# One of two attention output tiles goes to the shared PSUM banks, and four operand tiles of the channel mixing become float32 tiles

## The chip, the cores and the metric

The kernel runs on one core of one Trainium2 chip. The metric is the device time of one execution in microseconds. Before the change the median of three runs is 569.63 us (568.62 to 572.48).

## The reference

Two steps follow each other. The first is an attention without softmax in which weights decay with distance; `lam` is one decay factor per head. The second mixes over the positions ("token mixing") and then over the features ("channel mixing").

```python
# q, k, v: (4 batches, 8 heads, 768 positions, 64), block of 64 positions
for b in range(nb):
    intra = einsum('bhic,bhjc->bhij', qb, kb) * Dmask      # lam ** (i - j) below the diagonal
    intra = einsum('bhij,bhjd->bhid', intra, vb)
    inter = einsum('bhic,bhcd->bhid', qb * lam_pow, kv_state)
    out[:, :, sl] = intra + inter
    kv_state = lam_block * kv_state + einsum('bhsd,bhse->bhde', kb * rev_pow, vb)

x  = out as (4, 768, 512)
h  = maximum(x.transpose(0, 2, 1) @ w_tok1, 0) @ w_tok2    # 768 -> 256 -> 768
u  = x + h.transpose(0, 2, 1)
h2 = maximum(u @ w_ch1, 0) @ w_ch2                         # 512 -> 1536 -> 512
return u + h2
```

All is float32. Where the kernel multiplies float32 matrices on TensorE in the faster fp32r type, it splits each operand into a high and a low part and adds three products.

## The kernel before

**Order.** There is one program, and each engine works through its own list of instructions in the order in which the Python code writes them. An instruction that must wait stops all that stand behind it on its engine. Tiles that bear the same tag in a pool share a fixed number of buffers in turn: a new tile takes the buffer that was taken longest ago, and its first write waits until the last reader of that buffer's previous tile is done. Nothing else sets the order.

**Attention (the loop at L618 to L700).** A pair is one batch and two heads; there are 16 pairs, and iteration `i` of the loop runs from -2 to 15. A sequence of 768 positions is six chunks of 128, and most tiles hold three chunks, so that each step comes as halves `g` = 0 and 1. On TensorE (PE) the iteration has, in this order:

- the scores of pair i+1 (`sc`, L287);
- the outputs of pair i, first half (`xT`, L314 for the weights times v, L324 for the part from the running state), which ScalarE (ACT) copies to `uT` at L331;
- the products k·v of pair i+1 (`kv`, L254), from which VectorE (DVE) makes the running states at L262 in one scan (`sv`);
- the outputs of pair i, second half (`xT` again);
- the transposes of k of pair i+2 in two tiles (`kt`, L211), copied by ACT at L216, and for the first pairs those of q (`qt`, L228, copied by ACT at L229); later pairs' q is transposed by DVE at L221;
- groups of the token mixing that are ready (`ph` L446, `pu` L467), and between them the outputs of pair i transposed back (`xp`, L346) and split by ACT (`xhi`, L354) and DVE (`xlo`, L355).

Between these the queue `waiting` puts steps that read weights in and split them; one such chain runs ACT L377, L378, DVE L379, L380, L383, ACT L390 for a piece.

**PSUM banks.** `bank` (L105) gives a tile with one of three tags: `sc` has four buffers, `xT` one, `sh` three. `kv`, `kt`, `qt`, `xp`, `ph` and `pu` take `sh` in turn; both halves of the outputs take the only `xT`.

**Channel mixing (L1256 to L1399).** It runs over n = 0 to 17 (three rounds of six), with seven products each (`product`, L783, into PSUM banks `a`, `b`, `d`; at L797 TensorE writes them). After a product comes its `drain` (L820): ACT and DVE take the bank, add, apply the maximum, and make pairs of operand tiles, a high and a low part (`hi_of` on ACT, at L812; `low_of` on DVE, at L808; `low_sum` on GpSimd (POOL), at L818). The second weight matrix is applied by `mm2` (L998) in the first round, and by `half` (L1037, products `gb` and `gc` at L1052) in the other two. POOL also splits second weights (`c2hx`, `c2lx`, at L1127) and operands (`o3l` to `o7l`, at L583, shared with DVE).

Two queues hand out tiles there, first in, first out: `tiles` holds operand tiles (fp32r), which `hi_of` takes in pairs and `half` gives back; `temps` holds float32 tiles for sums on the way (`snap`, `e` of L837, `temp`), which are given back by `give`. Which tile of a queue an instruction uses depends on how many are in it. All tiles stand in SBUF.

Of the kernel before, what the change touches and what calls it, by code (L numbers as in the profile page):

```python
# [9 lines left out]
F32 = mybir.dt.float32  # L10
F32R = mybir.dt.float32r
# [14 lines left out]
def kernel(  # L26
# [28 lines left out]
    P = 128  # L55
# [6 lines left out]
    CB = 512  # L62
# [8 lines left out]
    def later(n, at_end=False):  # L71
        left = 0 if at_end and len(waiting) < 8 else 1 + (n > 2)
        n += len(waiting) > 7
        for _ in range(min(n, len(waiting))):
            left -= waiting[0] in acts
            if left < 0 and n < 99:
                break
            waiting.popleft()()
# [26 lines left out]
    def bank(tag, nm, n):  # L105
        return ps.tile([P, n], F32, tag=tag, bufs={"sc": 4, "xT": 1, "sh": 3}[tag], name=nm)
# [199 lines left out]
    def outputs(i, g):  # L306
        b, p = pairs[i]
        st = stb[i % 2]
        xT = bank("xT", f"xT{i}{g}", 3 * P)
        for cg in range(3):  # L310
            c = 3 * g + cg
            cs = slice(cg * P, (cg + 1) * P)
            for h in range(2):
                nc.tensor.matmul(  # L314
                    out=xT[h * D : (h + 1) * D, cs],
                    lhsT=vns[i][:, h, c, :],
                    rhs=weights_of[i, g, h][:, cg, :],
                    start=(cg == 0),
                    stop=False,
                )  # L320
            if c == 0:
                continue
            for h in range(2):
                nc.tensor.matmul(  # L324
                    out=xT[h * D : (h + 1) * D, cs],
                    lhsT=st[:, c - 1, h, :],
                    rhs=qss[i][:, c - 1, :],
                    start=False,
                    stop=(cg == 2),
                )  # L330
        nc.scalar.copy(out=uT[b][:, p, 3 * g * P : (3 * g + 3) * P], in_=xT)  # L331
# [286 lines left out]
    for i in range(-2, NI):  # L618
# [8 lines left out]
        if i >= 0:  # L627
            outputs(i, 0)
# [3 lines left out]
        if i >= 0:  # L632
            outputs(i, 1)
        if i + 2 < NI:
            turn_q(i + 2)
        if i in loads:
            x = loads.index(i)
# [43 lines left out]
        if i in turns:  # L681
            x = turns.index(i)
# [84 lines left out]
    def flush():  # L767
        for f in todo.popleft() if todo else []:
            f()
# [13 lines left out]
    def product(n, s):  # L783

        r, g = divmod(n, NG)
        o = PROD[s]
        ch, cl = c1s[n]
        oh, ol = ops[r, o]
        c = c_of.setdefault(n, {})
        into = {1: "b", 2: "a", 6: "b", 7: "d", 5: "b", 3: "b", 4: "d"}[o]  # L790
        if into not in c:
            c[into] = bank("sc", f"{into}{n}", CB)
        first = o in (1, 2, 7)
        i = 0
        for ct in range(2):
            for w, x in ((ch, oh), (cl, oh), (ch, ol)):
                nc.tensor.matmul(  # L797
                    out=c[into], lhsT=w[:, WI[o], ct], rhs=x[:, ct], start=(first and i == 0), stop=(i == 5),
                    skip_group_check=True,
                )  # L800
                i += 1

    tiles, temps, ring, G = deque(), deque(), deque(), {}
# [178 lines left out]
    def mm2(n, x, t):  # L982

        r, g = divmod(n, NG)
        if n < NG:
            c2h, c2l = c2s[n]
            cs = slice(t * P, (t + 1) * P)
            po = bank("sh", f"po{n}{x}{t}", CB)
        else:
            w2 = W[n, t // 2]  # L990
            c2h, c2l = w2[:, 0], w2[:, 1]
            cs = slice(t % 2 * P, (t % 2 + 1) * P)
            po = list(G.values())[(4 * x + t) % 4]
        i = 0
        for jj in range(JG):
            hh, hl = hs[n, jj, x]
            for w, h in ((c2h, hh), (c2l, hh), (c2h, hl)):
                nc.tensor.matmul(out=po, lhsT=w[:, jj, cs], rhs=h, start=(i == 0), stop=(i == 3 * JG - 1), skip_group_check=n >= NG)  # L998
                i += 1
            if t == 3 and n >= NG:  # L1000
                tiles.extend((hh, hl))
        if n >= NG and x == 0 and t % 2 == 1:
            spent(n, t // 2)
        return lambda: gather(n, x, t, po)
# [197 lines left out]
    def later2(n):  # L1202
        for _ in range(min(n, len(fuse))):
            if fuse[0]() is False:
                break
            fuse.popleft()
# [16 lines left out]
    def convert(g, i):  # L1223
        at = dict(name=f"wa{g}{i}")
        if len(pieces) % 3 == 0:
            a = wp.tile([P, 4 * FG], U32, tag="wa", bufs=1, **at)
        else:
            a = fp.tile([P, 4 * FG], F32, tag="fa", bufs=2, **at).bitcast(U32)
        fresh[g, i] = a.bitcast(F32)
        t = wp.tile([P, 4 * FG], U32, tag="t", bufs=1, name=f"t{g}{i}")  # L1230
        waiting.extend(convert_piece(fresh[g, i, 0], a, signs, t))
        waiting.append(lambda: converted.add((g, i)))
# [9 lines left out]
    def next_piece():  # L1242
        if pieces:
            raw_of(*pieces[0])
# [11 lines left out]
    for n in range(NQD):  # L1256
        r, g = divmod(n, NG)
        for s in range(7):
# [22 lines left out]
            if n == 0:  # L1281
# [12 lines left out]
                if s == 0:  # L1294
                    p2.close()
                    hp = ctx.enter_context(tc.tile_pool(name="hp", bufs=3, reuse_waits="tile"))
# [12 lines left out]
            if n < NG:  # L1309
                for q_ in range(s, s + 1 if s < 6 else 8):  # L1310
                    if q_ == s:
                        product(n, s)
                        flush()
                        later(1)
                        later2(2)
                        if sums:
                            sums.popleft()()
                        drain(n, s)
                    add = mm2(n - 1, 1 - q_ // 4, q_ % 4)
                    flush()  # L1320
                    later(1)
                    later2(2)
                    add()
                    if n < NG and pieces:
                        if tick in turn_at:
                            convert(*pieces.popleft())
                        if tick - 2 in turn_at:
                            next_piece()
                        tick += 1
            else:  # L1330
                if n == NG and s == 0:
                    tasks.extend(lambda q_=q_: mm2(NG - 1, 1 - q_ // 4, q_ % 4) for q_ in range(8))
                if n == NG and s == 1:
                    for i in range(4):
                        x = tp.tile([P, 2, CB], F32R, tag="tt", bufs=4, name=f"tt{i}")
                        tiles.extend((x[:, 0], x[:, 1]))
                if n == NG + 1 and s == 1:
                    for i in range(3):
                        for t in ("hh0", "hl0", "hh1", "hl1"):
                            tiles.append(hp.tile([P, CB], F32R, tag=t, name=f"{t}x{i}"))  # L1340
                    for t in ("c2h", "c2l"):
                        x = w2b.tile([P, JG, DM], F32R, tag=t, name=f"{t}x")
                        ring.append(x.rearrange("p a (j e) -> p a j e", j=JG))
                    pump()
                    for t in range(2):
                        G["b", t] = bank("sh", f"gb{t}", CB)
                    G["c", 0] = bank("sh", "gc0", CB)
                    G["c", 1] = bank("xT", "gc1", CB)
                if n % 2 and n < NQD - 2 and s == 2:
                    tasks.extend(lambda o=o, i=i, d=n // 2: half(d, o, i) for o in ORDER for i in range(2))  # L1350
                if n == NQD - 1 and s == 0:
                    tasks.extend(lambda q_=q_: mm2(NQD - 2, 1 - q_ // 4, q_ % 4) for q_ in range(8))
                if r == 1 and n % 2 == 0 and s == (0 if n == NG else 3):
                    take_raw(n // 2)
                    fuse.extend(sums_of_weights(n // 2))
                product(n, s)
                flush()
                if sums:
                    sums.popleft()()
                drain(n, s)  # L1360
                later2(1)
                k = (1, 1, 2, 1, 2, 1, 2)[s] if n == NQD - 1 else 1
                for _ in range(k):
                    add = tasks.popleft()() if tasks else lambda: None
                    flush()
                    later2(1)
                    add()
                    if todo_out:
                        todo_out.popleft()()
# [4 lines left out]
        if n == NG - 1:  # L1374
# [8 lines left out]
            for t in ("c2h", "c2l"):  # L1383
                x = wa.tile([P, JG, DM], F32R, tag=t, name=f"{t}x")
# [42 lines left out]
```

## Time and profile before

| what | value |
|---|---|
| median of the runs | 569.63 us (568.62 to 572.48) |
| the profiled execution, its own time | 567.56 us |
| its span in the trace | 565.8 us, so 1.76 us lie around it |
| PE busy in the span | 541.0 us (96%) |
| DVE, POOL, ACT busy | 387.8, 285.4, 247.3 us |
| mean granted TensorE clock | 0.995 of full speed |

The times of the trace count from the start of the span. A row of the timeline gives the start, the busy time, the engine, the line, the operation, the tile written and the tiles read, the shape, how many instructions it groups, and in brackets how long the engine stood idle before and what ended that. In a table of windows the columns are the window, then per engine the busy time with the number of instructions in brackets (PE, its weight loads, DVE, ACT, POOL), the granted clock, the DMA share and GB/s. Weight loads run beside matmuls, so that PE busy and PE weight loads overlap.

### The profile page before, as it was taken

Reading aid. Unit: us, or ns where it says so; the run is one execution under the profiler, and the core shown is the slowest. Engines: PE = TensorE matmul, PEld = TensorE weight load, DVE = VectorE, ACT = ScalarE, POOL = GpSimd, SP = SyncE. Lnnn points to the kernel's source line nnn. Section 1 sums busy time; section 2 is a strip of 40 time slices with the busy share of each in tenths; the row PEclk is TensorE's granted clock in tenths of the full one; section 3 lists DMA queues with packets and bytes.
Section 4 is the critical chain, followed back from the end, with each engine's and each line's share of the span. In section 5 each row is a group of like instructions: output and inputs, shape, how many; then the busy total and the mean of one; then the engine's idle time right before and its main releaser. Section 6 shows DMA issues by size and latency. Waiting matters only on the chain.

```text
span 565.8 us, 9630 instructions
## 1 busy us (share of the span) xinstructions
PE 541.0 (96%) x3686; PEld 459.9 (81%) x3686; DVE 387.8 (69%) x590; ACT 247.3 (44%) x449; POOL 285.4 (50%) x240
## 2 busy tenths in 40 slices
PE   5987989999999999999999999999998999999996
PEld 4877879988998988888888878888876888888884
DVE  4747776676684787888896667389479765575463
ACT  3456543453524546456445344343465334332111
POOL 6746548345324287667639753385788223131000
PEclk9989999999999999999999999999999999999999
DMA  9999887199630158687587999868536797653007
GB/s 183 248 228 209 189 192 170 30 228 216 133 71 2 74 205 311 221 286 279 189 294 238 259 213 252 308 218 311 181 104 223 156 234 280 240 182 137 0 3 146
DMA packets 163726, 108.12 MB, mean 191 GB/s; under 512 B 136800, under 2 KB 147552, under 8 KB 163680
## 3 DMA queue, kind: packets, MB, share of 16 engines
q1 hardware_dynamic: 153648, 87.31, 58.6%
q10 hardware_dynamic: 10032, 20.19, 9.7%
q8 instruction: 29, 0.48, 0.3%
q14 instruction: 17, 0.14, 0.1%
HBM read 75.50 MB, written 31.98 MB: 190 GB/s over the span
## 4 chain that ended last, share of the span: by engine, by line
PE 81%; DVE 6%; ACT 4%; issue 2%; DMA 2%; SPq 1%; POOL 1%; ACTq 1%; DVEq 0%; POOLq 0%
PE b L797 16%; PE po L998 11%; PE gb L1052 9%; PE d L797 8%; PE gc L1052 6%; PE ph L446 6%; PE pu L467 5%; PE a L797 4%; PE xT L314 4%; PE sc L287 3%; PE xT L324 2%; PE gb L998 2%; PE gc L998 2%; DMA qn<-in_q_dram 1%; PE xp L346 1%
## 5 line engine op out<-in xcount | busy, mean ns | idle before, releaser
L275 POOL COPY stb<-sv 64x320 f32<-64x320 f32 x32 | 25.4, 793 | 50.7 <-DVE sv L262 49.7
L314 PE MATMUL xT<-a,vn 128*64 128x128 f32 x384 | 37.1, 285 | 5.2 <-ACT uT L331 5.2
L331 ACT COPY uT<-xT 128x384 f32<-128x384 f32 x32 | 15.4, 480 | 55.5 <-PE xT L324 55.5
L1011 DVE TENSOR_TENSOR uT<-po,uT 128x512 f32<-128x512 f32 x48 | 32.6, 683 | 10.2 <-PE po L998 10.0
L998 PE MATMUL po<-hh,c2l 128*128 128x512 f32 x96 | 37.7, 393 | 0.0
L998 PE MATMUL po<-hl,c2h 128*128 128x512 f32 x96 | 37.6, 392 | 0.0
L998 PE MATMUL po<-hh,c2h 128*128 128x512 f32 x96 | 37.6, 391 | 0.0
L300 DVE TENSOR_TENSOR a<-sc,mask 128x384 f32<-128x384 f32 x64 | 32.1, 543 | 4.9 <-PE sc L287 4.9
L324 PE MATMUL xT<-qs,stb 128*64 128x128 f32 x320 | 32.0, 278 | 0.0
L818 POOL TENSOR_TENSOR tt<-t,tt 128x512 fp32r<-128x512 f32 x13 | 16.8, 1296 | 29.1 <-ACT tt L812 27.2
L314 PEld LDWEIGHTS xT<-a,vn 128*64 128x64 f32 x384 | 22.7, 139 | 9.3 <-ACT uT L331 6.0
L1067 DVE TENSOR_TENSOR uT<-gb,uT 128x512 f32<-128x512 f32 x40 | 26.1, 683 | 3.8 <-PE gb L1052 3.8
L446 PE MATMUL ph<-xhi,w1h 128*128 128x256 f32 x96 | 28.2, 294 | 0.3 <-DVE hl L451 0.3
L355 DVE TENSOR_TENSOR xlo<-xp,xhi 128x384 fp32r<-128x384 f32 x32 | 17.7, 554 | 14.7 <-ACT xhi L354 14.6
L287 PE MATMUL sc<-qT,kT 64*128 64x128 f32 x384 | 26.5, 286 | 0.8 <-DVE qT L221 0.5
L446 PE MATMUL ph<-xlo,w1h 128*128 128x256 f32 x96 | 27.1, 283 | 0.0
L446 PE MATMUL ph<-xhi,w1l 128*128 128x256 f32 x96 | 27.1, 283 | 0.0
L287 PEld LDWEIGHTS sc<-qT,kT 64*128 64x128 f32 x384 | 23.4, 193 | 3.9 <-issue 1.7
L525 POOL TENSOR_TENSOR c1l<-wa,c1h 128x512 fp32r<-128x512 f32 (+1 forms) x12 | 18.7, 1569 | 15.6 <-ACT c1h L522 15.6
L818 POOL TENSOR_TENSOR hl1x<-t,hh1x 128x512 fp32r<-128x512 f32 x12 | 16.8, 1404 | 18.9 <-ACT hh1x L812 18.3
L241 POOL TENSOR_TENSOR qs<-qT,lamp 128x640 f32<-128x640 f32 x16 | 25.4, 1589 | 0.0
L797 PE MATMUL b<-o,c1h 128*128 128x512 f32 x72 | 25.2, 391 | 0.0
(359 smaller groups left out, 1724.8 us busy)
## 6 DMA issues: line engine op xcount, KB each, us to landing
c1h<-k SPq DMA_DIRECT2D x12, 896.0 KB, 5.6
c1l<-k SPq DMA_DIRECT2D x12, 896.0 KB, 8.1
raw<-in_moe_w_ch_dram SPq DMA_DIRECT2D x7, 1024.0 KB, 6.0
kn<-in_k_dram SPq DMA_DIRECT2D x32, 192.0 KB, 4.5
vn<-in_v_dram SPq DMA_DIRECT2D x16, 384.0 KB, 5.8
k<-c1h ACTq DMA_DIRECT2D x6, 896.0 KB, 3.6
k<-c1l ACTq DMA_DIRECT2D x6, 896.0 KB, 4.2
out_dram<-y SPq DMA_DIRECT2D x80, 64.0 KB, 2.4
```

The source lines that it names most:

```text
L287: nc.tensor.matmul(out=sc[h][:, c * P : (c + 1) * P], lhsT=kTs[i][r, cs], rhs=qTs[i][r, cs], start=True, stop=True,)
L300: nc.vector.tensor_mul(out=a, in0=scored[i, g][h].rearrange("p (c i) -> p c i", i=P), in1=mask[:, 2 * p + h, None, :].broadcast_to([P, 3, P]),
L314: nc.tensor.matmul(out=xT[h * D : (h + 1) * D, cs], lhsT=vns[i][:, h, c, :], rhs=weights_of[i, g, h][:, cg, :], start=(cg == 0), stop=False,)
L324: nc.tensor.matmul(out=xT[h * D : (h + 1) * D, cs], lhsT=st[:, c - 1, h, :], rhs=qss[i][:, c - 1, :], start=False, stop=(cg == 2),)
L446: nc.tensor.matmul(out=ph, lhsT=w[:, c, fs], rhs=x[:, c], start=(i == 0), stop=(i == 3 * NC - 1))
L467: nc.tensor.matmul(out=pu, lhsT=h[:, kk, cs], rhs=w[:, kk, ss], start=(i == 0), stop=(i == 3 * NK - 1))
L797: nc.tensor.matmul(out=c[into], lhsT=w[:, WI[o], ct], rhs=x[:, ct], start=(first and i == 0), stop=(i == 5), skip_group_check=True,)
L818: nc.gpsimd.tensor_sub(out=B_[key][1], in0=src, in1=B_[key][0].bitcast(F32))
L998: nc.tensor.matmul(out=po, lhsT=w[:, jj, cs], rhs=h, start=(i == 0), stop=(i == 3 * JG - 1), skip_group_check=n >= NG)
L1011: nc.vector.tensor_add(out=ub, in0=two(po), in1=ub)
L1052: nc.tensor.matmul(out=G[into, t], lhsT=w2[:, v, j, t * P : (t + 1) * P], rhs=x, start=(o in (5, 1, 2) and not second and i == 0), stop=(i ...
L1067: nc.vector.tensor_add(out=ub, in0=two(G[into, t]), in1=ub)
```

## The change

Two places change. The second half of a pair's outputs takes a buffer of `sh` in place of the `xT` buffer. And of the twelve tiles with tags `hh0`, `hl0`, `hh1`, `hl1` that are added in the channel mixing at n = 7, the last four go as float32 tiles to `temps` in place of fp32r tiles to `tiles`. `tiles` then hands out 16 operand tiles in place of 20 from there on, `temps` 13 in place of 9.

```diff
     def outputs(i, g):
         b, p = pairs[i]
         st = stb[i % 2]
-        xT = bank("xT", f"xT{i}{g}", 3 * P)
+        xT = bank("sh" if g else "xT", f"xT{i}{g}", 3 * P)
...
                 if n == NG + 1 and s == 1:
                     for i in range(3):
                         for t in ("hh0", "hl0", "hh1", "hl1"):
-                            tiles.append(hp.tile([P, CB], F32R, tag=t, name=f"{t}x{i}"))
+                            at = dict(tag=t, name=f"{t}x{i}")
+                            if i < 2:
+                                tiles.append(hp.tile([P, CB], F32R, **at))
+                            else:
+                                temps.append(hp.tile([P, CB], F32, **at))
```

Every engine has the same instructions in the same order as before; what changes is the buffers they use and with that what they wait for. The first place is TensorE in iteration 2, from the end of `kv3` on: `xT21` is the second half of pair 2's outputs, `kt40` and `kt41` the transposes of k of pair 4, `qt40` the first of q. In brackets stand the semaphores that a first instruction waits for. Before:

```order
L254 MATMUL kv3_517<-vn3_351,kd3_459 64x64 x8
L314 MATMUL xT21_534<-a210_406,vn2_233 64x128 [waits Activation_49]
...
L324 MATMUL xT21_534<-qs2_375,stb0_111 64x128 x2
L211 MATMUL kt40_550<-ident_61,kn4_353 128x128 [waits DMAHW7_49,DMAHW6_49,DVE_49]
L211 MATMUL kt40_550<-ident_61,kn4_353 128x128 x2
L211 MATMUL kt41_555<-ident_61,kn4_353 128x128 [waits DVE_49]
L211 MATMUL kt41_555<-ident_61,kn4_353 128x128 x2
L228 MATMUL qt40_560<-ident_61,qn4_354 128x128 [waits DMAHW1_49,DMAHW0_49,DVE_49]
```

And now:

```order
L254 MATMUL kv3_517<-vn3_351,kd3_459 64x64 x8
L314 MATMUL xT21_534<-a210_406,vn2_233 64x128 [waits DVE_49]
...
L324 MATMUL xT21_534<-qs2_375,stb0_111 64x128 x2
L211 MATMUL kt40_550<-ident_61,kn4_353 128x128 [waits DMAHW7_49,DMAHW6_49,DVE_49]
L211 MATMUL kt40_550<-ident_61,kn4_353 128x128 x2
L211 MATMUL kt41_555<-ident_61,kn4_353 128x128 [waits DVE_49]
L211 MATMUL kt41_555<-ident_61,kn4_353 128x128 x2
L228 MATMUL qt40_560<-ident_61,qn4_354 128x128 [waits DMAHW1_49,DMAHW0_49,Activation_49]
```

`xT21` no longer waits for ACT, which copies the first half out of the `xT` bank. With one more tile in the turn of `sh`, each tile behind it takes another buffer: of the three buffers in use before `kv3`, `xT21` takes the one that stood first in line for `kt40`, `kt40` the one that stood next, `kt41` that of `kv3` itself (whose reader is the scan `sv3` on DVE), and `qt40` that of `xT21` (whose reader is ACT's copy).

The second place is DVE in iteration n = 11 of the channel mixing, at its sum `e` (L837), with `d11` the bank of a product. Before:

```order
L1069 TENSOR_TENSOR uT_60<-uT_60,gc1_3912 128x512 [waits DVE_49,PE_49]
L583 TENSOR_TENSOR o7l2_4527<-uT_60,o7h2_4526 128x512 [waits Activation_49]
L837 TENSOR_TENSOR snap1_3667<-d11_4498,t1_3661 128x512 [waits DMAHW0_49,DMAHW6_49,Activation_49,Pool_49]
L808 SCALAR_TENSOR_TENSOR t0_3660<-snap1_3667,t0_3660 128x512 [waits DVE_49]
L583 TENSOR_TENSOR o5l2_4552<-uT_60,o5h2_4551 128x512 [waits PE_49,Activation_49]
L808 SCALAR_TENSOR_TENSOR hl0x2_3904<-snap1_3667,hh0x2_3903 128x512
```

And now:

```order
L1069 TENSOR_TENSOR uT_60<-uT_60,gc1_3912 128x512 [waits DVE_49,PE_49]
L583 TENSOR_TENSOR o7l2_4527<-uT_60,o7h2_4526 128x512 [waits Activation_49]
L837 TENSOR_TENSOR t0_3660<-d11_4498,snap0_3666 128x512 [waits DVE_49,Activation_49]
L808 SCALAR_TENSOR_TENSOR hl0x2_3904<-t0_3660,hl0x2_3904 128x512 [waits DVE_49,Pool_49]
L583 TENSOR_TENSOR o5l2_4552<-uT_60,o5h2_4551 128x512 [waits PE_49,Activation_49]
L808 SCALAR_TENSOR_TENSOR tt2_3707<-t0_3660,tt2_3707 128x512
```

The sum `e` writes another tile, `t0` in place of `snap1`, and no longer waits for POOL or for DMA queues; the rows around it stand in the same order.

## The prediction

> **What bounds the kernel now.** I read the page's busy shares and chain first, then a table of windows to see where TensorE stands idle, then the list of TensorE's waits, then the timeline at each.
>
> ```profile
> PE 541.0 (96%) x3686; PEld 459.9 (81%) x3686; DVE 387.8 (69%) x590; ACT 247.3 (44%) x449; POOL 285.4 (50%) x240
> ...
> PE 81%; DVE 6%; ACT 4%; issue 2%; DMA 2%; SPq 1%; POOL 1%; ACTq 1%; DVEq 0%; POOLq 0%
> ```
>
> ```profile
> 31.60:130.00 98.40, 88.58 (x1081) 81.08 (x1078) 69.19 (x117) 50.02 (x101) 54.70 (x52) 0.98 0.84 175
> ...
> 184.00:413.00 229.00, 228.75 (x1030) 189.34 (x1030) 172.27 (x238) 109.29 (x185) 144.74 (x109) 1.00 0.73 239
> 413.00:440.00 27.00, 24.82 (x106) 19.23 (x105) 22.48 (x30) 16.23 (x31) 22.49 (x15) 1.00 0.48 161
> ```
>
> TensorE is busy for 541.0 of 565.8 us, so all idle time together is 24.8 us, the most that taking waits away can give. Of that 98.40 - 88.58 = 9.8 lies in the attention and 27.00 - 24.82 = 2.2 where the change of the queues acts. From 184 to 413 it is idle for 0.25 of 229: what TensorE gains before, it keeps there.
>
> ```profile
> PE xT L314 <- ACT uT L331: 5.2, 4, 2.1
> ...
> PE gc L1052 <- DVE hl0x L808: 1.0, 1, 1.0
> PE gb L1052 <- DVE uT L1067: 0.6, 1, 0.6
> PE gc L1052 <- DVE tt L808: 0.5, 1, 0.5
> ```
>
> The first edit aims at 5.2 us in four stalls; the second touches the stretch of the other three, 2.1 together.
>
> **First edit: the outputs' second half in the shared banks.** The wait for ACT's copy goes in all pairs, but every tile behind it in the rotation shifts. `kt` of the second half now lands on the buffer of `kv`, which is free when DVE's scan `sv` ends; before, it waited for something older, and the tile after `kt` (`qt`, `xp` or `pu`) waited for the scan. So the scan is what comes late next, one `kt` earlier in TensorE's queue. Iteration 2 has the longest stall:
>
> ```profile
> 31.45 0.89 PE L254 MATMUL kv<-vn,kd 128*64 128x64 f32 x20
> 34.44 0.69 PE L314 MATMUL xT<-a,vn 128*64 128x128 f32 x4 [2.09 <-ACT uT L331]
> ...
> 38.16 0.95 PE L228 MATMUL qt<-ident,qn 128*128 128x128 f32 x6
> ```
>
> ```profile
> 33.90 0.48 ACT L331 COPY uT<-xT 128x384 f32<-128x384 f32 x1
> ```
>
> ```profile
> 34.04 0.56 DVE L355 TENSOR_TENSOR xlo<-xp,xhi 128x384 fp32r<-128x384 f32 x1 [1.06 <-ACT xhi L354]
> ...
> 35.44 0.81 DVE L262 TENSOR_TENSOR_SCAN sv<-keep,kv 128x320 f32<-128x320 f32 x1
> ```
>
> ```profile
> 24.90 0.44 PE L314 MATMUL xT<-a,vn 128*64 128x128 f32 x4
> ...
> 26.36 0.87 PE L211 MATMUL kt<-ident,kn 128*128 128x128 f32 x6
> 27.07 1.01 PE L228 MATMUL qt<-ident,qn 128*128 128x128 f32 x6
> ```
>
> ```profile
> 30.93:34.34 3.41, 1.42 (x34) 1.28 (x30) 2.31 (x5) 1.90 (x5) 0.63 (x1) 1.00 1.14 229
> 34.35:37.75 3.40, 3.31 (x27) 2.98 (x28) 2.81 (x6) 0.47 (x2) 3.34 (x4) 0.50 0.98 182
> ...
> 41.18:44.58 3.40, 2.06 (x46) 1.80 (x42) 2.30 (x5) 1.86 (x5) 0.72 (x1) 1.00 1.04 383
> ```
>
> The copy ends at 34.38, late because ACT's queue had splits of a weight and of `xp` ahead. The granted clock then reads 0.50 for 3.4 us, right after a window with 1.42 us of TensorE work; a window with 2.06 kept the clock. At full clock the half takes 26.36 - 24.90 = 1.46 us, and both `kt` 27.07 - 26.36 = 0.71.
>
> After the change the half runs from 32.34 to about 33.8. The first `kt` waits for `xlo` (34.04 + 0.56 = 34.60) and ends at 34.96. The second waits for the scan (35.44 + 0.81 = 36.25, some 0.05 to the start) and starts near 36.3; `qt` follows at 36.3 + 0.36 = 36.66 instead of 38.16. That is 1.5 us less, provided that the clock drops before and not after: then 0.8 + 1.3 us of idle time stand in two pieces with work before, between and behind, and the window from 34.35 holds about 0.4 + 1.4 = 1.8 us of work, nearer to 2.06 than to 1.42. Without the drop the old order would have reached `qt` at 34.44 + 1.46 + 0.71 = 36.61, so the edit alone gives nothing here: all of the 1.5 is clock.
>
> The Trainium skill (TensorE: Matmul & The Clock Gate, Part 1: The HAM clock gate) puts the fall to half rate after at least one idle window of about 3.4 us. The trace goes further: 2.09 us idle was enough. By the page's rule alone no stall here would cost clock, and the sum below would be +0.1. The same section says that the window runs freely, so that runs differ; one profiled run cannot show this, and it is the first rival.
>
> Iteration 3, and what the others do:
>
> ```profile
> 44.59 0.44 PE L314 MATMUL xT<-a,vn 128*64 128x128 f32 x4 [1.35 <-ACT uT L331]
> ...
> 46.05 0.87 PE L211 MATMUL kt<-ident,kn 128*128 128x128 f32 x6
> ```
>
> ```profile
> 45.59 0.81 DVE L262 TENSOR_TENSOR_SCAN sv<-keep,kv 128x320 f32<-128x320 f32 x1
> ```
>
> The scan ends at 46.40; the second `kt` started at 46.05 + 0.36 = 46.41 before. The stall of 1.35 goes and turns up again ahead of that `kt`: nothing gained. The third stall, 5.2 - 2.09 - 1.35 - 0.58 = 1.18 in iteration 4, is of the same kind, 0. The last has no `kt` and no scan behind it, so its 0.58 is won:
>
> ```profile
> 180.16 0.44 PE L314 MATMUL xT<-a,vn 128*64 128x128 f32 x4 [0.58 <-ACT uT L331]
> ```
>
> Two iterations lose, since a `kt` that hid part of the scan now waits for it:
>
> ```profile
> 65.00 0.87 PE L211 MATMUL kt<-ident,kn 128*128 128x128 f32 x6
> 67.16 0.55 PE L346 MATMUL xp<-ident,uT 128*128 128x128 f32 x3 [1.29 <-DVE sv L262]
> ```
>
> ```profile
> 66.29 0.81 DVE L262 TENSOR_TENSOR_SCAN sv<-keep,kv 128x320 f32<-128x320 f32 x1
> ```
>
> ```profile
> 126.09 0.88 PE L211 MATMUL kt<-ident,kn 128*128 128x128 f32 x6
> 127.83 0.44 PE L467 MATMUL pu<-w2h,hh 128*128 128x384 f32 x1 [0.87 <-DVE sv L262]
> ```
>
> ```profile
> 126.97 0.80 DVE L262 TENSOR_TENSOR_SCAN sv<-keep,kv 128x320 f32<-128x320 f32 x1
> ```
>
> In iteration 5 `xp` started when the scan ended; now the second `kt` starts then and pushes `xp` by 0.36. Iteration 10 is the same with `pu`, 0.36. In the others the scan ends before the second `kt` would start, by the same comparison. Sum: -1.5 + 0 + 0 - 0.58 + 0.36 + 0.36 = -1.4. Its bounds: -6.9 if all 5.2 is won and with it half of a 3.4 us window; +2.0 if the clock drops after the change in iterations 2 and 5 (-1.4 + 2 x 1.7). I take -1.4, as each wait has its row.
>
> **Second edit: four operand tiles become float32 tiles.** No instruction moves. Fewer operand tiles could make ACT wait at L812 until a product gives one back:
>
> ```profile
> ACT tt L812 <- DVE a L837: 9.9, 4, 3.0
> ```
>
> Among ACT's waits from 384 us on, those of L812 are all for DVE, this the largest, so a tile that comes back up to some 3 us later is not felt: 0. More float32 tiles take away one wait of DVE for POOL:
>
> ```profile
> 419.08 1.84 POOL L1127 TENSOR_TENSOR c2lx<-snap,c2lx 128x512 fp32r<-128x512 f32 x1
> 420.87 1.30 POOL L583 TENSOR_TENSOR o7l<-uT,o7h 128x512 fp32r<-128x512 f32 x1
> 422.13 1.75 POOL L1127 TENSOR_TENSOR c2hx<-t,c2hx 128x512 fp32r<-128x512 f32 x1
> ```
>
> ```profile
> 420.95 0.69 DVE L837 TENSOR_TENSOR snap<-d,t 128x512 f32<-128x512 f32 x1 [1.19 <-POOL c2lx L1127]
> 421.68 1.04 DVE L808 SCALAR_TENSOR_TENSOR t<-snap,t 128x512 f32<-128x512 f32 x1
> 422.85 1.57 DVE L583 TENSOR_TENSOR o5l<-uT,o5h 128x512 fp32r<-128x512 f32 x1
> 424.35 0.68 DVE L808 SCALAR_TENSOR_TENSOR hl0x<-snap,hh0x 128x512 fp32r<-128x512 f32 x1
> ```
>
> ```profile
> 425.08 0.50 PE L1052 MATMUL gc<-hl0x,c2hx 128*128 128x512 f32 x1 [1.02 <-DVE hl0x L808]
> ```
>
> The sum at 420.95 can start at 419.76, and a plain shift would bring `hl0x` and so `gc` 1.2 us earlier. But the rows of POOL and DVE read as turns. POOL's 422.13 row lasts 1.75 where 420.87 took 1.30, and ends at 423.88, 1.16 after DVE's 421.68 row ends (422.72); DVE's 422.85 row lasts 1.57 and ends at 424.42, 0.54 after POOL's end. Each waits for the other, a turn of POOL about 1.15, one of DVE 0.55 to 0.65. Replayed from the end of the POOL row at 420.92: DVE `t` to 421.5, POOL `o7l` to 422.65, DVE `o5l` to 423.2, POOL `c2hx` to 424.35, DVE `hl0x` to 425.0, against 425.03 before. POOL's operations between stay the same in number, so I take 0; the bounds are -2.2, all idle time of the stretch, and +1.2, one more turn of POOL ahead of `hl0x`.
>
> The Trainium skill (SBUF — State Buffer, Who interferes with whom) describes this as an exclusive lock between a GpSimd operation that reads SBUF and a VectorE operation with two SBUF inputs, held for the whole instruction. The trace agrees, 1.75 against 1.30. By the rule the early start is worth 0, by the plain shift -1.2.
>
> **The rivals.** *The clock drop is not in the timed runs.* It shows in one execution, which at 567.56 is faster than all three timed ones; against that, the window's 1.42 us of work is far below the 2.06 that passed. Then iteration 2 gives 0 and the edits 0.36 + 0.36 - 0.58 = +0.1: 569.8. *The second edit pays too.* If DVE takes its turn ahead of POOL's `c2hx`, `hl0x` ends at 423.2 + 0.65 = 423.85, -1.2: 569.6 - 1.4 - 1.2 = 567.0. *Slower: the new waits cost the clock.* In iteration 5 TensorE now idles from 65.36 to 67.16, 1.8 us, between the 1.35 that kept the clock and the 2.09 that lost it; in iteration 2 the two pieces together are 2.1. It decides where a clock window holds less work than some 1.4 to 2.06. Both lost: +2.0, 571.6; for it speaks the closeness, against it that each idle piece is shorter than 2.09. *Nothing reaches the end*: DVE, busy for 172 of the 229 us from 184 on, paces some of that stretch and takes the gain back: 569.6; against it stands TensorE's 0.25 idle. *All is won*: the scan is not waited for, the clock stays, the second edit clears its stretch: -6.9 - 2.1 = -9.0, 560.6; the scan's rows speak against it.
>
> **How the numbers follow.** The profiled execution took 567.56, 1.76 beyond its span, and would take 566.2 with -1.4. The median is 2.1 above it; I carry the difference over: 569.6 - 1.4 = 568.2. Chances: forecast 0.40; no drop in the timed runs 0.25; second edit pays 0.15; clock lost 0.10; nothing reaches the end 0.05; all won 0.05. The range leaves out the last and the clock's loss, 0.15; it runs from 567.0 to 569.8 and 1.0 further at each end, which is what the two nearest runs of before differ by: 566.0 to 570.8. About 1% is what a measurement of this kernel can tell from no change, 5.7 us. Only the case of all won is faster by that, with some of its neighbourhood 0.06; slower by that would need the clock lost in several places more, 0.03.
>
> **What would show it.** The four waits for `uT` L331 are gone from TensorE's list and waits of `kt` L211 for `sv` stand in iterations 2 to 5 and 10; the clock reads 1.00 through 34 to 38; `qt` of iteration 2 starts near 36.7; DVE's `e` starts near 419.8 less the shift of 1.4, and `gc` still waits for `hl0x` about 1 us. A drop of clock behind one of the new waits, or a DVE chain that comes earlier by a full 1.2, would prove the forecast wrong.

## The result and the profile after

The changed kernel takes 566.21 us (median of 22 runs, 564.15 to 572.56) against 569.76 us of the kernel before in runs beside it (565.91 to 574.35). The ratio is 0.995, with a 95% interval of 0.9929 to 0.9971, that is 1.7 to 4.0 us less. In a second comparison further below it was 0.998 (0.996 to 1.0001). The profiled execution has a span of 562.4 us against 565.8. The forecast was 568.2, 1.4 below before: the direction was right and the time in the range, but the gain was more than forecast.

TensorE's waits in the changed kernel (us in total, times, longest):

```profile
PE kt L211 <- DVE sv L262: 6.6, 5, 1.8
...
PE kt L211 <- DVE xlo L355: 1.3, 2, 1.0
...
PE gc L1052 <- DVE tt L808: 0.9, 1, 0.9
...
PE gc L1052 <- DVE hl0x L808: 0.5, 1, 0.5
```

The four waits for the copy are gone, and five waits for the scan, together longer, stand in their place. The windows say the same:

```profile
31.60:130.00 98.40, 87.20 (x1085) 80.30 (x1085) 70.96 (x120) 51.02 (x102) 56.38 (x53) 1.00 0.86 177
...
413.00:440.00 27.00, 24.97 (x107) 19.29 (x106) 24.57 (x32) 14.23 (x28) 20.95 (x14) 1.00 0.52 163
```

Between 31.6 and 130 TensorE is now idle for 11.2 us, 1.4 more than before, yet the kernel is shorter. So the gain is not in what the tables list as idle time. Iteration 2 on TensorE goes as worked out, 0.3 us late by its start:

```profile
34.97 0.55 PE L211 MATMUL kt<-ident,kn 128*128 128x128 f32 x3 [1.03 <-DVE xlo L355]
36.62 0.55 PE L211 MATMUL kt<-ident,kn 128*128 128x128 f32 x3 [1.11 <-DVE sv L262]
37.01 0.82 PE L228 MATMUL qt<-ident,qn 128*128 128x128 f32 x6
```

I set the TensorE instructions of the two traces against each other in order and followed how far each starts earlier than before. The places at which this shift steps:

| place (time before) | shift ahead | shift behind | step | forecast |
|---|---|---|---|---|
| iteration 2 (31.5 to 37.8) | +0.28 | -1.21 | -1.5 | -1.5 |
| iterations 3 and 4 | -1.21 | -1.10 | +0.1 | 0 |
| iteration 5 (65 to 67) | -1.26 | -0.66 | +0.6 | +0.36 |
| iteration 10 (126 to 128) | -1.64 | -1.17 | +0.5 | +0.36 |
| iteration 15 (180) | -2.02 | -2.82 | -0.8 | -0.58 |
| pairs 1 and 5 to 14, at the second half of the outputs | | | -0.16 to -0.27 each, -2.2 in all | 0 |
| 334 us | -2.82 | -3.29 | -0.5 | 0 |
| 425 us | -3.29 | -3.48 | -0.2 | 0 |

The table starts late by 0.28: up to 31.4 us the changed kernel stood 0.1 ahead, and then `kv` waited 0.2 us for ACT (`kd`, L236), which put it back by 0.4. The first profile of the kernel before has no such wait, the two further ones below have it, so it does not belong to the change.

Two things remain to be explained: the small steps in the eleven pairs, and whether the 1.5 us of iteration 2 are there in every execution. (The step at 334 us is a stall of 0.26 us in the first profile of the kernel before; a second profile of the same kernel, below, lacks as much, so it does not belong to the change.)

Here is one of the eleven, iteration 7. Before, TensorE and then ACT:

```profile
89.41 0.75 PE L254 MATMUL kv<-vn,kd 128*64 128x64 f32 x20
90.16 0.44 PE L314 MATMUL xT<-a,vn 128*64 128x128 f32 x4
```

```profile
89.63 0.48 ACT L331 COPY uT<-xT 128x384 f32<-128x384 f32 x1 [3.54 <-PE xT L324]
```

And TensorE after:

```profile
88.48 0.75 PE L254 MATMUL kv<-vn,kd 128*64 128x64 f32 x20
89.06 0.39 PE L314 MATMUL xT<-a,vn 128*64 128x128 f32 x4
```

The second half can follow 0.58 us behind the start of `kv`. Before, it started 0.75 behind, 0.05 after ACT's copy ended (89.63 + 0.48 = 90.11). This is a wait of 0.17 us that no view lists: matmuls overlap in the pipeline (in the rows after, `kv` counts as busy until 89.23 and `xT` starts at 89.06), and before the change the last of `kv` still counts as busy until 90.16.

### The profile page after: what moved, and what is told of

Same layout as the page of the kernel before. It is cut to its first block, busy times and chain, and to the rows that moved or that the text cites. A ratio compares the mean times of both kernels' runs of the same rounds, so it can differ in the third digit from the quotient of the medians.

```text
span 562.4 us, 9620 instructions
## 1 busy us (share of the span) xinstructions
PE 537.3 (96%) x3686; PEld 457.7 (81%) x3686; DVE 389.3 (69%) x590; ACT 247.2 (44%) x449; POOL 286.0 (51%) x240
## 4 chain that ended last, share of the span: by engine, by line
PE 86%; DVE 7%; ACT 3%; DMA 2%; issue 1%; SPq 0%; ACTq 0%; DVEq 0%
PE b L797 17%; PE po L998 12%; PE gb L1052 9%; PE d L797 8%; PE gc L1052 7%; PE ph L446 6%; PE pu L467 5%; PE a L797 4%; PE sc L287 3%; PE xT L314 3%; PE xT L324 2%; PE gb L998 2%; PE gc L998 2%; DMA uT<-in_moe_w_tok_dram 2%; PE kt L211 1%; PE kv L254 1%
## 5 line engine op out<-in xcount | busy, mean ns | idle before, releaser
L314 PE MATMUL xT<-a,vn 128*64 128x128 f32 x384 | 35.8, 277 | 0.0
L324 PE MATMUL xT<-qs,stb 128*64 128x128 f32 x320 | 31.5, 273 | 0.0
L818 POOL TENSOR_TENSOR hl1x<-t,hh1x 128x512 fp32r<-128x512 f32 x7 | 9.3, 1330 | 40.0 <-ACT hh1x L812 40.0
L211 PE MATMUL kt<-ident,kn 128*128 128x128 f32 x96 | 15.7, 294 | 13.6 <-DVE sv L262 6.6
L797 PE MATMUL a<-o,c1h 128*128 128x512 f32 x72 | 25.2, 390 | 0.0
```

Source lines behind the costliest of these rows:

```text
L314: nc.tensor.matmul(out=xT[h * D : (h + 1) * D, cs], lhsT=vns[i][:, h, c, :], rhs=weights_of[i, g, h][:, cg, :], start=(cg == 0), stop=False,)
L324: nc.tensor.matmul(out=xT[h * D : (h + 1) * D, cs], lhsT=st[:, c - 1, h, :], rhs=qss[i][:, c - 1, :], start=False, stop=(cg == 2),)
L797: nc.tensor.matmul(out=c[into], lhsT=w[:, WI[o], ct], rhs=x[:, ct], start=(first and i == 0), stop=(i == 5), skip_group_check=True,)
```

## The experiments

Theory A: the gain is the first edit's. It consists of the clock in iteration 2 and of the covered waits, while the listed waits only change their place. Theory B: the second edit pays a part. Theory C: only listed waits count, as forecast.

### Each edit alone

First the first edit only:

```diff
-        xT = bank("xT", f"xT{i}{g}", 3 * P)
+        xT = bank("sh" if g else "xT", f"xT{i}{g}", 3 * P)
```

> First edit alone, in all pairs. Theory A (the gain is the first edit: the clock of iteration 2, plus 0.17 to 0.22 us in each pair whose copy of the first half outlasts the products k.v without showing as idle time): TensorE stands 2.8 us earlier than before at the end of the attention, and the execution is 2.8 us shorter, ratio 0.995. Theory B (both edits pay, the second some 0.6 of the 3.4 us of span): 2.2 to 2.8 us shorter, and the stall of 0.26 at 334 us and the one of 1.02 at 425 us are as before. Theory C (only the four listed waits count, as forecast): 1.4 us shorter.

Measured: 565.09 us against 567.66, ratio 0.9967 (0.9948 to 0.9986), so 0.8 to 3.0 us less. In its trace the shift stands 1.9 to 2.0 us ahead of before at the end of the attention, less than the 2.8 expected, and the reason is in the clock of iteration 5:

```profile
64.00:66.00 2.00, 0.53 (x5) 0.54 (x6) 2.00 (x5) 0.14 (x1) 0.52 (x1) 1.00 1.52 172
66.00:68.00 2.00, 2.00 (x15) 2.00 (x13) 1.74 (x3) 1.95 (x5) 1.52 (x3) 0.69 1.47 161
68.00:70.00 2.00, 2.00 (x12) 2.00 (x11) 0.03 (x1) 0.68 (x2) 1.89 (x2) 0.50 0.67 110
```

Behind the new wait of 1.8 us the granted clock falls to 0.50, and the shift goes from -1.30 to +0.09: the rival "the new waits cost the clock", in one of its two places, at 1.4 us.

Then the second edit only:

```diff
-                            tiles.append(hp.tile([P, CB], F32R, tag=t, name=f"{t}x{i}"))
+                            at = dict(tag=t, name=f"{t}x{i}")
+                            if i < 2:
+                                tiles.append(hp.tile([P, CB], F32R, **at))
+                            else:
+                                temps.append(hp.tile([P, CB], F32, **at))
```

> Second edit alone. Theory A: DVE's sum e no longer waits 1.2 us for POOL, but the two engines take turns and TensorE's product gc still waits 0.9 to 1.0 us, so 0 to -0.2 us. Theory B: -0.6 us or, by a plain shift of the chain, -1.2. Iteration 2 is as before, so the granted clock should again read about 0.50 for one window of 3.4 us behind the stall of 2.1; if it reads 1.00 the drop belongs to single executions.

Measured: 567.81 against 567.66, ratio 1.0001 (0.9968 to 1.0034). TensorE's waits there are 0.9 (for `tt`) and 0.5 (for `hl0x`), as in the changed kernel, in place of 1.0 and 0.5. The time alone leaves 1.8 us either way open. The trace decides: a shift of the chain by 1.2 us would show at 425 us, and the step there is -0.2. So theory B falls by the trace, and the second edit is worth 0.1 to 0.2 us. DVE's sum `e` starts without a wait there too. Iteration 2 reads 0.50 once more, and near 87 us the clock falls a second time.

### The eight quiet pairs

```diff
-        xT = bank("xT", f"xT{i}{g}", 3 * P)
+        xT = bank("sh" if g and i in (6, 7, 8, 9, 11, 12, 13, 14) else "xT", f"xT{i}{g}", 3 * P)
```

> The first edit in the eight pairs 6, 7, 8, 9, 11, 12, 13, 14 alone, none of which has a listed wait for the copy or a scan that ends late. Theory A: each gains about 0.19, in all -1.5 us, and the shift against before grows in eight steps of 0.17 to 0.27. Theory C: 0, since no row of idle time goes away. Iteration 2 is as before: one more look at the clock there, 0.50 expected.

Measured: 566.51 against 567.66, ratio 0.9987 (0.9965 to 1.0009). The time alone does not tell -1.5 from 0 (-2.0 to +0.5). The trace does: from 31.6 us, where the shift is +0.78, it goes down to -0.80 behind pair 14, by 1.58 us, at the second halves of just these pairs, while TensorE's list keeps the same waits for `uT`:

```profile
PE xT L314 <- ACT uT L331: 5.2, 4, 2.1
```

```profile
90.02 0.75 PE L254 MATMUL kv<-vn,kd 128*64 128x64 f32 x20
90.60 0.39 PE L314 MATMUL xT<-a,vn 128*64 128x128 f32 x4
```

The second half follows `kv` by 0.58 instead of 0.75. So theory A holds for these pairs, and C falls: about 0.2 us in each came from a wait that no list shows. (Later stalls behind the attention, 1.2 and 1.0 us for copies by ACT, are in this execution and not in that of the kernel before; they mask the step in its span.)

### Pair 2 alone, and the clock

```diff
-        xT = bank("xT", f"xT{i}{g}", 3 * P)
+        xT = bank("sh" if g and i == 2 else "xT", f"xT{i}{g}", 3 * P)
```

> The first edit in pair 2 alone. Theory A: -1.5 us where the clock drops in the order before, since the wait moves from the copy to the scan and only the clock is won; -0.1 where it does not drop. If the clock drops in nearly every execution, the median is about 1.5 lower; if in half of them, about 0.7. Rival: the waits add up as listed, -2.1.

Measured: 568.01 against 567.66, ratio 0.9996 (0.997 to 1.0021): at best 1.7 us of gain, so the rival's 2.1 is out. Its trace has the clock at 1.00 in iteration 2 and the shift steps by -1.36 there (+0.55 to -0.81). One trace has nearly the whole 1.5 us, and the median nothing measurable, which suggests that the clock differs between executions. So the kernel before was profiled twice more, unchanged.

> The kernel before once more, for its profile. If the clock behind the stall of 2.1 us drops in nearly every execution: about 0.50 for 3.4 us in iteration 2. If it is a matter of single executions: 1.00 there, and the span is shorter by 1.5 us for that.

> The kernel before, a further look at the clock behind the 2.1 us stall. Of four looks at that order so far three read 0.5 to 0.55 there and one 1.00. A clock window whose start runs freely gives either; 1.00 with a stall whose idle time is split between two windows.

Both have the same stall of 2.09 us, from 33.0 to 35.1 in the second profile of the kernel before and from 33.7 to 35.8 in the third. The windows shown are those of a grid that is worked out right behind them. The second profile:

```profile
30.76:34.17 3.41, 1.93 (x36) 1.44 (x32) 2.19 (x4) 1.90 (x4) 0.00 (x0) 1.00 1.12 236
34.17:37.58 3.41, 2.48 (x33) 2.26 (x33) 2.88 (x6) 1.78 (x6) 3.21 (x3) 1.00 1.03 190
```

The third profile:

```profile
31.91:35.32 3.41, 1.28 (x24) 0.85 (x20) 2.19 (x4) 1.91 (x6) 0.30 (x1) 1.00 1.19 242
35.32:38.73 3.41, 2.98 (x25) 2.65 (x26) 3.13 (x6) 0.48 (x3) 3.35 (x4) 0.50 0.83 158
```

The same code with the same stall: 1.00 in one execution, 0.50 in another. What differs is where the stall falls in a grid of windows. In each profile the stretches at half clock start a whole multiple of 3.413 us apart: 34.34 and 563.41 in the first profile (155 of them; the second is the drop when TensorE has ended), 35.32 and 86.52 in the third (15). Where a profile has only the drop at its end, the grid follows from that one, as in the second (563.24, 155 windows behind 34.17). The grid lies elsewhere in each execution. Cut into these windows, from about 10 us to the end of the matmuls, the twelve profiles of this case agree: all 23 windows with 1.68 us of PE busy time or less (eleven inside the kernel, twelve at its end) are followed by half clock, and none of the 1914 windows with 1.75 us or more is. Half a window, 1.71 us, lies between. The second profile's stall is split, with 1.93 us of work in its poorest window; of the third's, 1.7 us lie in one window, which holds 1.28 us of work.

The second profile's span is 564.4 us against 565.8 and 567.8 (the third lost the clock a second time near 87 us). In the old order the clock fell in iteration 2 in four of five profiles (three of the kernel before, the second edit alone, the quiet pairs).

The changed kernel was also run again:

> The changed kernel once more, beside the other kernels. Ratio 0.995 to 0.997 to the kernel before. Its profile: if the clock's window runs freely, the wait of 1.8 us in iteration 5 may now lower the granted clock to about 0.5 for 3.4 us, which it did not in the first profile.

Measured: 566.65 against 567.65, ratio 0.998 (0.996 to 1.0001). This profile lost the clock in both places:

```profile
36.00:39.00 3.00, 2.51 (x12) 2.51 (x13) 1.35 (x3) 1.25 (x3) 2.84 (x4) 0.58 1.03 170
...
68.00:70.00 2.00, 2.00 (x11) 2.00 (x11) 1.16 (x2) 1.91 (x4) 1.48 (x2) 0.50 0.86 162
```

Its shift goes from -1.34 to +0.07 in iteration 2 and from +0.11 to +1.57 in iteration 5. With the new order the clock fell in iteration 2 in two of six profiles and in iteration 5 in three of four. These are few profiles, but the direction is plain: the change makes a drop rarer in one place and risks one in another. What is left without any clock is the difference of two profiles with no drop, 562.4 of the changed kernel against 564.4 of the second one before: 2.0 us, close to the sum of the steps without iteration 2 (-2.2 - 0.8 - 0.2 + 0.1 + 0.6 + 0.5 = -2.0).

### The scan's wait: leave pairs 5 and 10 out, or give kv its own bank

```diff
-        xT = bank("sh" if g else "xT", f"xT{i}{g}", 3 * P)
+        xT = bank("sh" if g and i not in (5, 10) else "xT", f"xT{i}{g}", 3 * P)
```

> Both edits, but pairs 5 and 10 keep the xT bank for both halves. Theory A: 2 x 0.36 us won back, 2 x 0.19 lost, so 0.35 us below the changed kernel, and with the wait of 1.8 us in iteration 5 the drop of the clock there (seen in the first edit alone) is gone in the executions that have it, worth 1.4 to 1.7 us each.

Measured: 565.02 against 567.65, ratio 0.9973 (0.9942 to 1.0004), and 1.6 below the changed kernel's 566.65, with intervals that overlap. Its trace keeps the clock at 1.00 in iteration 5, which one profile can't show to be the rule. In it the shift at the end of the attention is -3.4 instead of -2.8, a gain of 0.6 over the changed kernel, where 0.35 was expected; the difference is smaller than what the time resolves.

The other kernel swaps the banks, so that no tile behind `kv` lands on the buffer that the scan reads:

```diff
-        kv = bank("sh", f"kv{i}", D * (NC - 1))
+        kv = bank("xT", f"kv{i}", D * (NC - 1))
...
-        xT = bank("sh" if g else "xT", f"xT{i}{g}", 3 * P)
+        xT = bank("sh", f"xT{i}{g}", 3 * P)
```

> Both edits, but the products k.v take the single bank with the tag xT, and both halves of the outputs take the three shared banks. No tile behind kv then lands on the buffer that the scan reads. Theory A (the scan's wait took the place of the copy's, 6.6 us in five places): the waits of kt for the scan go; of them the ones in iterations 2, 4, 5 and 10 (some 1.3 + 1.1 + 1.8 + 1.2) become shorter programs, the one of iteration 3 comes back as a wait of the scores for DVE's transposed q: 4 to 5 us below the changed kernel. Rival (DVE, with scan and masks in its queue, sets the pace of these iterations anyway): the waits return at other tiles, within 1 us of the changed kernel.

Measured: 561.41 us (560.23 to 563.3) against 567.65, ratio 0.99 (0.9875 to 0.9924), and 5.2 below the changed kernel's 566.65 in the same comparison. It beats both kernels. Its TensorE waits:

```profile
PE kt L211 <- DMA kn<-in_k_dram: 5.7, 1, 5.7
PE sc L287 <- DVE qT L221: 1.8, 1, 1.8
PE pu L467 <- DVE xlo L355: 1.2, 1, 1.2
PE ph L446 <- DVE xlo L355: 1.0, 1, 1.0
```

```profile
31.60:130.00 98.40, 90.89 (x1114) 83.42 (x1112) 72.55 (x123) 50.70 (x103) 58.60 (x53) 1.00 0.86 181
```

All waits for the scan are gone. In iteration 4 nothing takes their place; iteration 3 comes back as expected, as a wait of the scores for DVE's transposed q (0.6 in the changed kernel, 1.8 now). The others come back in part, at other tiles: 0.8 for 2.1 in iteration 2 (`kt` for ACT's copy), 1.0 for 1.8 in iteration 5 (`ph` for `xlo`), 0.9 for 1.4 in iteration 10 (`pu` for DVE's `uT`), and `kv` waits twice for POOL, 0.7 together. TensorE is idle for 7.5 us in this stretch, 3.7 less than in the changed kernel. The rival (DVE sets the pace anyway, within 1 us) falls: the span of this profile is 3.4 us shorter than the changed kernel's first (559.0 against 562.4), and neither has a drop of the clock before its end. That the rest of the 5.2 is drops in the changed kernel was not shown. So a part of what held the first edit's gain back is this: one buffer further in the rotation, and the next tile waits for the slowest reader.

### The turns of POOL and DVE

Two subtractions of POOL, the low part of one second weight and half of one operand's, become fills with zero; these parts of the result are left out.

```diff
-        eng.tensor_sub(out=two(ol[:, ct]), in0=src, in1=two(oh[:, ct]).bitcast(F32))
+        if r == 2 and o == 5 and eng is nc.gpsimd:
+            eng.memset(ol[:, ct].bitcast(F32), 0.0)
...
+                if (d, nm) == (5, "S3"):
+                    V.memset(hi[:, 1].rearrange("p j e -> p (j e)").bitcast(F32), 0.0)
```

> Both edits, and two of POOL's subtractions near 420 us (the low part of one second weight, c2hx at L1127, and half of one operand's, o5l at L583) become fills with zero of the same tiles, so that POOL writes as much but reads nothing there; the results of these parts are left out. Turn theory (POOL and DVE shut each other out while both read SBUF): DVE's tt, 1.78 us in the changed kernel, takes about 0.7, and the stalls of gc there (0.87 and 0.53 us) fall together by 0.9 to 1.4 us. Rival (the chain is set by ACT and DVE alone, and the long durations have another cause): 1.78 and 0.87 stay.

In the changed kernel, DVE and then POOL, at this place:

```profile
416.36 0.68 DVE L837 TENSOR_TENSOR t<-d,snap 128x512 f32<-128x512 f32 x1
...
419.77 1.78 DVE L808 SCALAR_TENSOR_TENSOR tt<-t,tt 128x512 fp32r<-128x512 f32 x1
```

```profile
419.26 1.74 POOL L1127 TENSOR_TENSOR c2hx<-t,c2hx 128x512 fp32r<-128x512 f32 x1
420.96 1.74 POOL L583 TENSOR_TENSOR o5l<-uT,o5h 128x512 fp32r<-128x512 f32 x1
```

With the fills:

```profile
422.64 0.68 DVE L811 SCALAR_TENSOR_TENSOR tt<-t,tt 128x512 fp32r<-128x512 f32 x1
```

```profile
422.11 0.52 POOL L1131 MEMSET c2hx<- 128x512 f32 x1
422.58 0.53 POOL L584 MEMSET o5l<- 128x512 f32 x1
```

```profile
PE gc L1055 <- DVE hl0x L811: 0.7, 1, 0.7
```

DVE's `tt` takes 0.68 instead of 1.78 beside a POOL that writes the same tiles without reading. Of TensorE's two stalls, 0.87 and 0.53, one of 0.7 is left, so together 0.65 are gone, less than the 0.9 to 1.4 expected, since the next `hl0x` then came late by itself. The turn theory holds for the durations: DVE's `tt` was long beside a POOL that reads. The fills are also shorter than the subtractions (0.5 against 1.7 us), but the fill of `o5l` runs from 422.58 to 423.11, beside `tt`, and does not lengthen it. The changed kernel's rows and these are from one profile each, and the time of this kernel, 566.13 us, is that of a single execution, so it shows no gain or loss.

## Why the prediction was right or wrong

**The first edit in the pairs that wait.** Right in mechanism. The waits for the copy went and came back as waits of `kt` for the scan, in iterations 2 to 5 and 10, as named; iterations 3 and 4 gave nothing (+0.1), and 15 gave 0.8 where 0.58 was forecast. Iterations 5 and 10 cost 0.6 and 0.5 instead of 0.36 each.

**The pairs that do not wait.** This is the step that failed. "In the others the scan ends before the second `kt` would start" is true, but it asks only what the edit adds there and takes for granted that nothing is won, because no wait was listed. Eleven pairs won 0.16 to 0.27 each, 2.2 us in all, more than the whole forecast. The rows for it were in the profile before: ACT's copy starts with the last output, lasts 0.48 and ends 0.7 behind the start of `kv`, whose twenty products need 0.58.

**The clock.** The drop behind the stall of 2.09 us was weighed as a matter of this one profile (chance 0.25 that it isn't in the timed runs). It is a matter of each execution: four of five in the old order, two of six in the new one. The prediction took the place of the clock's windows from one profile (30.93 to 34.34) as if it were fixed, and asked only what the window behind it would hold. With another grid the two pieces of idle time in iteration 2 share a window, 33.09 to 36.50 in the second profile of the changed kernel, which holds 1.31 us of work and loses the clock. Its bounds of 1.42 (lost) and 2.06 (kept) were right; the runs narrow them to 1.68 and 1.75. The rival "the new waits cost the clock" is real too, three of four in iteration 5, at 1.4 to 1.5 us each. So the -1.5 of iteration 2 is, by an estimate from these counts, about (4/5 - 2/6) x 1.5 = 0.7, and iteration 5 takes about 3/4 x 1.45 = 1.1 back. The old order also lost the clock near 87 us in two of five profiles. Over whole profiles it lost it six times in five, the new order with the first edit in all pairs five times in four, so by these few counts the clock gives nothing on balance. What is left is the 2.0 us of the other steps, which lies within the intervals of all three comparisons that have the first edit in all pairs (1.7 to 4.0, -0.1 to 2.3, and 0.8 to 3.0 for the first edit alone). It is more than the forecast's 1.4 because of the covered waits; the medians alone, from 1.0 to 3.6 us less, could not tell the two apart. The Trainium skill (TensorE: Matmul & The Clock Gate, Part 1: The HAM clock gate) calls the window free-running and the outcome run-variable; these runs agree, with 1.00 and 0.50 behind equal stalls. Its one idle window of about 3.4 us as the condition is not what they show: 1.8 us of waiting were enough in iteration 5, where a window held 1.56 us of work.

**The second edit.** Right. DVE's sum starts at once at 416.36 (forecast 419.8 less the shift), `gc` still waits 0.87 us, and the edit alone measured 1.0001 and moved its trace by 0.2. The fills agree with the turns that made it so.

**Rivals and range.** "The second edit pays too" would have given 567.0, which lies nearer to the measured 566.2 than the forecast's 568.2, and it is wrong all the same: the agreement of a time does not show its cause. The range, 566.0 to 570.8, held the time by 0.2 us, and that owes something to luck: 2.2 us of covered waits were not foreseen, and they were partly offset by a clock that on balance gave nothing where 1.5 was forecast.

## What to carry to other kernels

A wait on a buffer can hide in a pipelined engine: set the start of each consumer against the end of its buffer's last reader, in every iteration, before you price an edit at nothing. When a tile joins a rotation, look which reader the tiles behind it inherit, and give the tile with the slowest reader (here the scan's `kv`) the bank that is next used latest. Where a stall is near what lowers the clock, one profile is one throw: work out how little TensorE work a window can hold at any place of the grid, or profile several executions, before you count the clock as won.

## What the runs showed of the hardware that was not expected

With equal code and an equal stall of 2.09 us, the granted clock behind it read 1.00 in one execution and 0.50 in another; a wait of 1.8 us lowered it to 0.50 in three of four profiles. It is decided by the work in windows of 3.41 us, whose place differs from execution to execution: 1.68 us or less lost the clock for the next window, 1.75 or more kept it, in all twelve profiles. One such drop costs 1.3 to 1.5 us in this kernel. The version with `kv` in its own bank, which has one wait of 1.8 us left in the attention and kept the clock in its profile, ran between 560.23 and 563.3 us, while the kernel before spread from 565.44 to 573.53 in the same comparison; that the drops make up this spread was not shown.
